# Decode attention with a K/V cache: TensorE's loop rotated by one PV, with a new order of loads at the start and of VectorE's work at the end

## Chip, cores, metric

One Trainium2 chip, one of its cores. The metric is the time of one execution on the device in microseconds (us), the median over several executions. The chip of the first comparison gave 660.2 us for the kernel before.

## The reference

A transformer block for one new token, batch 2: layer norm, attention with 32 heads of 128 over a cache of 8192 keys and values per head, a residual, then a gated feed-forward layer.

```
h  = x + attention(layernorm(x), k_cache, v_cache, wq, wo)    # caches: [2, 32, 8192, 128] bf16
h2 = h + ffn(layernorm(h), W_gate, W_up, W_down)              # 512 -> 1376 -> 512
```

The caches are 2 x 134 MB of the 281 MB that the kernel reads. Arithmetic is small: each byte of the cache is used once.

## The kernel before

The work is cut into 32 pairs (two heads of one batch entry each). For each pair one K load and one V load of 4 MB go into four slots of on-chip memory: K of even pairs in slot 0, V of even pairs in 1, K of odd pairs in 2, V of odd pairs in 3. The scores of a pair are computed by two engines. VectorE takes 96 of the 128 columns (one multiply `k_mult`, four halving adds `k_adds`, one reduce), TensorE the other 32 (`k_part`: transposes, which ScalarE evicts, then small matmuls). ScalarE makes the exponentials. `pv` multiplies them with V on TensorE and adds up two pairs in one PSUM bank; ScalarE evicts the bank, that is, copies the results out of PSUM (`sums`), `collect` picks the results out of it, and VectorE divides by the sum of the exponentials (`normalize`, `o_scale`) and spreads the result for the output projection (`o_spread`). TensorE, VectorE and ScalarE run 15 turns of a loop, each one even and one odd pair. The last two pairs (30 and 31) are a straight tail, followed by the feed-forward layer. SyncE issues the loads in program order, each when its slot is free.

TensorE's loop and tail, with cuts:

```python
with nc.Fori(0, NI, engines=OrderedEngineSet([nc.tensor.engine])):
    k_part(body, 0, (1, 2, 3, 4), ((k2p, 1),))
    collect(body, 6)
    pv(body, 0, ((JC, J, ((slot_sem[1], 16), (a2p, 5))), (0, JC, ((a2p, 7),))))
    k_part(body, 1, (8, 9, 10, 11), ((k2p, 2),))
    nc.tensor.wait_ge(l2p, 1)
    o_gather(body)
    nc.tensor.sem_inc(l2p, -1)
    pv(body, 1, ((JC, J, ((slot_sem[3], 16), (a2p, 12))), (0, JC, ((a2p, EV),))))
    z_sum(Ob)
    nc.tensor.sem_inc(slot_sem[1], -16)
    nc.tensor.sem_inc(slot_sem[3], -16)
    nc.tensor.sem_inc(k2p, -2)
    nc.tensor.sem_inc(a2p, -EV)
n_body = pe.count - body.base
pe.count = body.base + NI * n_body

tail = Tokens(0)
P0, P1 = NP - 2, NP - 1
collect(tail, 1)
t_ob_loop = (pe.sem, tail.at["ob"])
k_part(tail, P0, (2, 3, 4, 5), ((k2p, 1),))
nc.tensor.wait_ge(l2p, 1)
o_gather(tail)
nc.tensor.wait_ge(a2p, 7)
nc.tensor.wait_ge(sem_wo, 16)
for r in range(DR):
    i = nc.tensor.matmul(
        Op[1][32 * (r % 4):32 * (r % 4) + B, :], lhsT=O_all[:, r, :], rhs=X[:, r * D:(r + 1) * D],
        start=(r < 4), stop=(r >= DR - 4))
tail.mark("op", i)
nc.tensor.wait_ge(a2p, 9)
for c in range(DC):
    nc.tensor.matmul(
        Wp[:, c * B:(c + 1) * B], lhsT=os_sb[:].rearrange("p (n c) -> p c n", c=DC)[:, c, :], rhs=sel2[:],
        start=False, stop=False, skip_group_check=True)
k_part(tail, P1, (10, 11, 12, 13), ((k2p, 2),))
pv(tail, P0, ((JC, J, ((slot_sem[1], 16), (a2p, 6))), (0, JC, ((a2p, 8),))))
pv(tail, P1, ((V_LAST, J, ((sem_vl[0], 16), (a2p, 15))), (0, V_LAST, ((a2p, 15), (sem_vl[1], 16)))),
   lambda: tail.mark("z", z_sum(Sp[0])))
```

PV, and what VectorE does for the last two pairs (P0 = 30, P1 = 31):

```python
def pv(T, p, parts, between=None):
    s = (2 * p + 1) % 4
    v_t = tile(s)
    q = p % PG
    n = 0
    for j0, j1, waits in parts:
        if between and n:
            nc.tensor.wait_ge(*waits[0])
            between()
        for sem, val in waits:
            nc.tensor.wait_ge(sem, val)
        for j in range(j0, j1, VJ):
            c = 32 * (n % 4)
            i = nc.tensor.matmul(
                Op[0][c:c + 16, :], lhsT=e_t[q][:, j // VJ, :],
                rhs=v_t[:, j:j + VJ, :].rearrange("p j d -> p (j d)"),
                start=(q == 0 and n < 4), stop=(q == PG - 1 and n >= J // VJ - 4))
            if T is body and n == 0:
                T.mark(("fp", p), i)
            n += 1
    T.mark(("pv", p), i)
# ...
    if p >= P0:
        nc.vector.wait_ge(g2d, p - P0 + 1)
        nc.vector.wait_ge(slot_sem[s], 16)
        nc.vector.sem_inc(k2p, 1)
        dve.last()
        t_dm[p] = dve.run(k_mult(p))
        k_adds(p, dve.run, dve.last)
        if p == P0:
            dve.wait(tokp("pv", p - 2))
        t_s[p] = dve.run(k_reduce(p))
        if p == P0:
            dve.wait(t_ob_loop)
            normalize(Ob, dve.run, dve.last)
            o_spread(g - 1, dve, dve.run(o_scale()))
```

ScalarE's part for pair 30 and the loads of SyncE:

```python
    if p == P0:
        act.wait(tokp("pv", p - 1))
        sums()
        evacs()
        act.wait(tok("og", NI))
        to_pe(nc.scalar.activation(
            out=O_all[:].rearrange("p r b -> p b r"),
            in_=Op[1][:, 0:B * DR].rearrange("p (b r) -> p b r", r=DR), func=ACT.Copy))
        act.wait(t_s[p])
        exp_dve(p)
        act.wait(tok("op", NI))
        to_pe(nc.scalar.activation(out=os_sb[:], in_=Op[1][:], func=ACT.Copy))
    elif p == P1:
        evacs()
        act.wait(t_s[p])
        exp_dve(p)

    if p + 2 < NP:
        sp.wait((d2s, p + 1), tokp("kf", p))
        load(s, A_k_cache, p + 2)
    v_loads = [p] if p < NP - 5 else [NP - 5] if p == NP - 4 else [NP - 4, NP - 3] if p == NP - 3 else []
    for r in v_loads:
        sp.wait(tokp("pv", r))
        if r < NP - 3:
            load((2 * r + 1) % 4, A_v_cache, r + 2)
# ...
```

The softmax here doesn't subtract the row's maximum and nothing guards it: scores larger than these inputs give would overflow.

## Time and profile before

| | kernel before |
|---|---|
| time, median of 6 runs | 660.2 us (660.03 to 660.39) |
| bytes read | 281 MB |
| one turn of the loop | 38.86 us |
| DMA rate in the loop | 432 GB/s, share 1.00 |
| VectorE busy in a turn | 28.8 us |
| TensorE busy in a turn | 18.7 us |

The table of stretches of the kernel before gives, for a stretch of time, the busy time of each engine, the granted clock of TensorE as a share of full speed, the busy share of the 16 DMA engines and what they moved. The first line is the columns, then one turn, then 11 turns.

```profile
core 0: us, PE busy (x) PEld busy (x) DVE busy (x) ACT busy (x) POOL busy (x), PEclk, DMA share, GB/s
92.05:130.89 38.84, 18.74 (x174) 10.85 (x174) 28.78 (x15) 12.84 (x26) 4.53 (x7) 0.59 1.00 432
130.89:558.36 427.47, 207.78 (x1914) 120.59 (x1914) 316.65 (x165) 141.45 (x286) 49.88 (x77) 0.58 1.00 432
```

No compute engine is busy for more than three quarters of a turn, and DMA is never idle. The chain of waits in order of time (start, us, what) says the same: it is made of K loads, each followed only by the multiply that frees its slot.

```profile
286.46 6.57 DVE prod L540
...
293.10 32.09 DMA slot<-in_A_k_cache_dram
...
325.31 6.57 DVE prod L540
```

A load of 4 MB at this rate takes 9.72 us (38.86 / 4). The list of DMA issues of the same profile (size, then median us from issue to landing) shows that K loads land after 32.1 us, so more than three loads are under way at once (32.1 / 9.72 = 3.3):

```profile
slot<-in_A_k_cache_dram SPq DMA_DIRECT2D x32, 4096.0 KB, 32.1
slot<-in_A_v_cache_dram SPq DMA_DIRECT2D x31, 4096.0 KB, 30.3
```

From the timeline of the kernel before (start, us, engine, instruction, and in brackets how long the engine was idle before it and for whom):

```profile
612.68 6.56 DVE L540 TENSOR_TENSOR prod<-slot,q_c 128x12288 bf16<-128x12288 bf16 x1 [0.92 <-DVEq L603]
616.70 3.33 PE L405 MATMUL O<-slot,e 128*16 128x512 bf16 x32 [13.06 <-DMA slot<-in_A_v_cache_dram]
...
620.73 1.05 PE L417 MATMUL Ob<-sel,os_sb 128*128 128x4 f32 x8 [0.39 <-ACT os_sb L569]
...
626.92 0.16 DVE L503 TENSOR_REDUCE zr<-Ob 128x4 f32<-128x8 f32 x1
...
628.02 6.55 DVE L540 TENSOR_TENSOR prod<-slot,q_c 128x12288 bf16<-128x12288 bf16 x1
...
641.05 6.08 PE L405 MATMUL O<-slot,e 128*16 128x512 bf16 x56
...
641.37 0.95 DVE L554 TENSOR_REDUCE scores<-prod 128x96 f32<-128x768 bf16 x1
...
647.38 0.61 PE L405 MATMUL O<-slot,e 128*16 128x512 bf16 x8
...
648.69 1.05 PE L417 MATMUL Ob<-sel,os_sb 128*128 128x4 f32 x8 [0.70 <-ACT os_sb L569]
...
657.22 0.65 SPq L820 DMA_DIRECT2D out_dram<-kT  x1
```

TensorE stands idle for 13.06 us until V of pair 29 lands, then does that PV and the collect. VectorE meanwhile goes through pairs 30 and 31 without a pause: the collect is done at 621.8, but `normalize` comes only at 626.92, behind the reduce of pair 30, so nobody waits for it. PV of pair 30 and most of PV of 31 are one run of 56 matmuls.

### The profile page before, as it was taken

How to read it: one execution, taken by the hardware profiler on the slowest of the kernel's cores; microseconds unless marked ns; L12 is line 12 of the kernel's file. 1: busy time of each engine (PE TensorE's matmuls, PEld its weight loads, DVE VectorE, ACT ScalarE, POOL GpSimd, SP SyncE). 2: the span in 40 equal slices, each digit the busy share in tenths (PEclk: the TensorE clock that was granted, in tenths of full speed). 3: DMA queues.
4: the chain of work that ended last, by engine and by line, in shares of the span. 5: the costliest groups of instructions: out<-in, count | busy, mean ns of one | idle time of the engine just before them, and what ended most of it. 6: DMA issues, size and time to landing. Idle time of an engine off the chain costs nothing.

```text
span 659.2 us, 7582 instructions
## 1 busy us (share of the span) xinstructions
PE 324.3 (49%) x3073; PEld 188.6 (29%) x3073; DVE 469.2 (71%) x280; ACT 213.6 (32%) x431; POOL 73.5 (11%) x125
## 2 busy tenths in 40 slices
PE   2753454435455343655535364443556444354577
PEld 0331332213233121433313142221324222133344
DVE  1585576788767678776768877676886767787991
ACT  1622333143342223334223343422324332333250
POOL 3002002020200202020020201002020110202000
PEclk9856556565756657555665756756555765655656
DMA  8999999999999999999999999999999999999997
GB/s 366 444 437 431 420 445 416 443 428 431 438 422 441 422 439 433 428 435 424 441 422 439 433 428 433 426 441 422 439 434 426 435 424 441 424 437 433 428 417 295
DMA packets 10653, 281.17 MB, mean 427 GB/s; under 512 B 1202, under 2 KB 1300, under 8 KB 1812
## 3 DMA queue, kind: packets, MB, share of 16 engines
q1 hardware_dynamic: 10632, 281.06, 99.3%
q8 instruction: 5, 0.08, 0.1%
q14 instruction: 4, 0.03, 0.0%
q10 hardware_dynamic: 12, 0.00, 0.0%
HBM read 281.05 MB, written 0.00 MB: 426 GB/s over the span
## 4 chain that ended last, share of the span: by engine, by line
DMA 76%; DVE 19%; PE 4%; issue 1%; ACT 1%; SPq 0%; DVEq 0%
DMA slot<-in_A_k_cache_dram 76%; DVE prod L540 16%; DVE prod L549 2%; PE O L405 1%; PE O L463 1%; PE T L381 0%; ACT kT L566 0%; PE W L469 0%; DVE scores L554 0%; PE S L756 0%; PE O L756 0%; PE O L808 0%; PE Ob L417 0%; SPq L172 0%; PE S L364 0%
## 5 line engine op out<-in xcount | busy, mean ns | idle before, releaser
L540 DVE TENSOR_TENSOR prod<-slot,q_c 128x12288 bf16<-128x12288 bf16 x32 | 209.9, 6558 | 148.0 <-DMA slot<-in_A_k_cache_dram 141.3
L405 PE MATMUL O<-slot,e 128*16 128x512 bf16 x1024 | 119.3, 621 | 219.9 <-ACT e L495 146.2
L549 DVE TENSOR_TENSOR prod<-prod 128x6144 bf16<-128x6144 bf16 (+3 forms) x128 | 212.2, 1657 | 7.8
L566 ACT ACTIVATE kT<-T 128x1024 bf16<-128x1024 bf16 x128 | 126.1, 1022 | 144.6 <-PE T L381 141.9
L381 PE MATMUL T<-ident_f,slot 128*128 128x128 f32 x512 | 108.6, 365 | 29.1 <-DVEq L587 29.1
L405 PEld LDWEIGHTS O<-slot,e 128*16 128x16 bf16 x1024 | 26.4, 114 | 287.0 <-ACT e L495 172.9
L495 ACT ACTIVATE e<-scores 64x96 bf16<-64x96 f32 x64 | 19.5, 304 | 239.6 <-DVEq L601 238.9
L381 PEld LDWEIGHTS T<-ident_f,slot 128*128 128x128 f32 x512 | 79.0, 188 | 44.2 <-DVEq L587 43.3
L537 POOL COPY q_c<-q_all 128x136 bf16<-128x136 bf16 x32 | 57.2, 1788 | 195.5 <-DVEq L591 152.5
L364 PE MATMUL S<-q_c,kT 128*128 128x4 bf16 x1024 | 47.4, 168 | 40.8 <-ACT kT L566 40.0
L364 PEld LDWEIGHTS S<-q_c,kT 128*128 128x128 bf16 x1024 | 39.1, 104 | 67.9 <-ACT kT L566 66.8
L417 PE MATMUL Ob<-sel,os_sb 128*128 128x4 f32 x136 | 30.1, 345 | 24.2 <-ACT os_sb L569 24.2
L417 PEld LDWEIGHTS Ob<-sel,os_sb 128*128 128x128 f32 x136 | 28.6, 311 | 26.1 <-ACT os_sb L569 26.1
L520 POOL MEMSET O_l<- 128x40 bf16 (+1 forms) x13 | 1.8, 136 | 303.9 <-DVEq L598 303.9
L554 DVE TENSOR_REDUCE scores<-prod 128x96 f32<-128x768 bf16 x32 | 30.5, 953 | 2.8
L566 ACT ACT_TABLE_LOAD x15 | 19.2, 1283 | 0.3
L495 ACT ACTIVATE e<-S 64x32 bf16<-64x32 f32 x64 | 13.0, 202 | 15.1 <-PE S L364 14.7
L569 ACT ACTIVATE os_sb<-O 128x512 f32<-128x512 f32 x17 | 10.1, 597 | 12.8 <-PE O L405 12.4
L495 ACT ACTIVATION_READ_ACCUMULATOR e<-S 64x1 f32 x64 | 12.8, 201 | 0.7
L495 ACT ACTIVATION_READ_ACCUMULATOR e<-scores 64x1 f32 x64 | 11.8, 185 | 0.0
L426 PEld LDWEIGHTS Ob<-zs,ones_f 128*128 128x128 f32 x30 | 7.1, 296 | 12.5 <-issue 12.5
L525 POOL COPY rsel<-rows 128x30 bf16<-128x30 bf16 x28 | 5.9, 209 | 33.3 <-DVEq L598 32.5
(104 smaller groups left out, 90.6 us busy)
## 6 DMA issues: line engine op xcount, KB each, us to landing
slot<-in_A_k_cache_dram SPq DMA_DIRECT2D x32, 4096.0 KB, 32.1
slot<-in_A_v_cache_dram SPq DMA_DIRECT2D x31, 4096.0 KB, 30.3
slot<-in_A_wq_dram SPq DMA_DIRECT2D x1, 4096.0 KB, 12.2
X<-in_A_wo_dram SPq DMA_DIRECT2D x1, 3840.0 KB, 45.8
slot<-in_A_v_cache_dram SPq DMA_DIRECT2D x1, 3072.0 KB, 23.3
slot<-in_B_W_up_dram SPq DMA_DIRECT2D x1, 1376.0 KB, 23.2
slot<-in_B_W_gate_dram SPq DMA_DIRECT2D x1, 1376.0 KB, 26.2
slot<-in_A_v_cache_dram SPq DMA_DIRECT2D x1, 1024.0 KB, 25.4
```

Source lines behind the costliest of these rows:

```text
L364: i = nc.tensor.matmul(Sp[p % 2][:, 2 * jj:2 * jj + 4], lhsT=kv_[:, k, r, :], rhs=q_c[p % 2][:, 4 * r:4 * r + 4], start=(r == 0), stop=(r ...
L381: i = nc.tensor.transpose(Tp[g % 2][:, k * 128:(k + 1) * 128], k_t[:, j:j + 2, :].rearrange("p j d -> p (j d)").bitcast(F32), ident_f[:])
L405: i = nc.tensor.matmul(Op[0][c:c + 16, :], lhsT=e_t[q][:, j // VJ, :], rhs=v_t[:, j:j + VJ, :].rearrange("p j d -> p (j d)"), start=(q == ...
L417: i = nc.tensor.matmul(Ob[:, 0:4], lhsT=os_sb[:, jj * Dh:(jj + 1) * Dh], rhs=sel[:, 4 * jj:4 * jj + 4], start=(jj == 0), stop=(jj == VJ - 1))
L426: return nc.tensor.matmul(bank[:, ZC:ZC + 8], lhsT=ones_f[:], rhs=zs[:], start=True, stop=True)
L495: i = nc.scalar.activation(out=e_t[q][h, j0 // VJ:j1 // VJ, 8 * q:8 * q + 8].rearrange("p g (j a) -> p g j a", a=2)[:, :, :, a], in_=src(h ...
L537: nc.gpsimd.tensor_copy(out=q_c[p % 2][:], in_=q_all[:, p]).then_inc(g2d, 1)
L540: return nc.vector.tensor_tensor(out=prod[:, 0:JC, :], in0=tile((2 * p) % 4)[:, 0:JC, :], in1=q_c[p % 2][:, 8:QW].unsqueeze(1).broadcast_t ...
L549: run(nc.vector.tensor_tensor(out=prod[:, 0:JC, 0:w], in0=prod[:, 0:JC, 0:w], in1=prod[:, 0:JC, w:2 * w], op=ALU.add))
L554: return nc.vector.tensor_reduce(out=scores[p % PG][:, 0:JC], in_=prod[:, 0:JC, 0:8], axis=AX.X, op=ALU.add)
L566: to_pe(nc.scalar.activation(out=kT[gg % 2][:], in_=Tp[gg % 2][:].bitcast(BF16), func=ACT.Copy))
L569: to_pe(nc.scalar.activation(out=os_sb[:], in_=Op[0][:], func=ACT.Copy))
```

## The change

The intent: TensorE should not hold up K of the next even pair by PV of the odd pair. So the loop begins with the sum and K of the even pair, and only then does PV of the odd pair of the turn before, its eviction and the collect. In the first turn that PV works on zeros (e is zero, slot 3 still holds wq, the sums are set to 1), so the result is not used. The slot of odd V is freed later, and the second V load is issued only in the first turn; wo is issued ahead of it. In the tail K of pair 30 also comes ahead of PV of 29, and VectorE does `normalize` and the spread behind its first add of pair 30, so that TensorE gets the spread early. Core of the diff, with cuts:

```diff
@@ -203,7 +203,11 @@
                     pool.run(nc.gpsimd.affine_select(
                         out=mask[:], in_=mask[:], pattern=[[2 * sgn, DR // 2], [-DR * sgn, NM]],
                         compare_op=ALU.is_ge, fill=0.0, base=base, channel_multiplier=sgn))
-                t_const = pool.run(nc.gpsimd.memset(zs[:], 0.0))
+                pool.run(nc.gpsimd.memset(zs[:], 0.0))
+                pool.last()
+                for a in range(2):
+                    t_const = pool.run(nc.gpsimd.memset(zs[64 * a:64 * a + 64, a:4:2, :], 1.0))
+                    pool.last()
                 dve.wait(t_id)
                 t_ident = dve.run(nc.vector.tensor_copy(out=ident[:], in_=ident_f[:]))
                 for bank in Op:
@@ -297,8 +301,6 @@
                     out=rows[:, 0:128 - 4 * DR], in0=rows[:, 0:128 - 4 * DR], in1=ident[:, 4 * DR:], op=ALU.max))
                 dve.last()
                 t_sel = dve.run(nc.vector.tensor_copy(out=rows[:, DR:], in_=rows[:, 0:DR]))
-                sp.wait(t_q)
-                load(3, A_v_cache, 1)
                 nc.sync.dma_start(
                     X[:], A_wo[0:128 * DR].rearrange("(p r) n -> p (r n)", r=DR)).then_inc(sem_wo, 16)
 
@@ -337,6 +339,7 @@
                 nc.tensor.matmul(Ob[:, 0:ZC + 8], lhsT=onesn[:], rhs=ident[:, 0:ZC + 8], start=True, stop=True)
 
                 EV = 13
+                nc.tensor.sem_inc(slot_sem[3], 16)
 
                 class Tokens:
 
... (pv and collect take the argument `done`, for whom they count)
@@ -434,15 +443,17 @@
                     T.mark("og", i)
 
                 with nc.Fori(0, NI, engines=OrderedEngineSet([nc.tensor.engine])):
-                    k_part(body, 0, (1, 2, 3, 4), ((k2p, 1),))
-                    collect(body, 6)
-                    pv(body, 0, ((JC, J, ((slot_sem[1], 16), (a2p, 5))), (0, JC, ((a2p, 7),))))
-                    k_part(body, 1, (8, 9, 10, 11), ((k2p, 2),))
+                    nc.tensor.wait_ge(a2p, 1)
+                    z_sum(Ob)
+                    k_part(body, 0, (2, 3, 4, 5), ((k2p, 1),))
+                    pv(body, 1, ((JC, J, ((slot_sem[3], 16),)), (0, JC, ())), done=p2a)
+                    collect(body, 7, ("pv", 1))
+                    pv(body, 0, ((JC, J, ((slot_sem[1], 16), (a2p, 6))), (0, JC, ((a2p, 8),))))
+                    k_part(body, 1, (9, 10, 11, 12), ((k2p, 2),))
                     nc.tensor.wait_ge(l2p, 1)
                     o_gather(body)
+                    nc.tensor.wait_ge(a2p, EV)
                     nc.tensor.sem_inc(l2p, -1)
-                    pv(body, 1, ((JC, J, ((slot_sem[3], 16), (a2p, 12))), (0, JC, ((a2p, EV),))))
-                    z_sum(Ob)
                     nc.tensor.sem_inc(slot_sem[1], -16)
                     nc.tensor.sem_inc(slot_sem[3], -16)
                     nc.tensor.sem_inc(k2p, -2)
@@ -452,12 +463,15 @@
 
                 tail = Tokens(0)
                 P0, P1 = NP - 2, NP - 1
-                collect(tail, 1)
+                nc.tensor.wait_ge(a2p, 1)
+                z_sum(Ob)
+                k_part(tail, P0, (2, 3, 4, 5), ((k2p, 1),))
+                pv(tail, P0 - 1, ((JC, J, ((slot_sem[3], 16),)), (0, JC, ())))
+                collect(tail, 7)
                 t_ob_loop = (pe.sem, tail.at["ob"])
-                k_part(tail, P0, (2, 3, 4, 5), ((k2p, 1),))
                 nc.tensor.wait_ge(l2p, 1)
                 o_gather(tail)
-                nc.tensor.wait_ge(a2p, 7)
+                nc.tensor.wait_ge(a2p, 8)
                 nc.tensor.wait_ge(sem_wo, 16)
                 for r in range(DR):
                     i = nc.tensor.matmul(
@@ -469,9 +483,9 @@
                     nc.tensor.matmul(
                         Wp[:, c * B:(c + 1) * B], lhsT=os_sb[:].rearrange("p (n c) -> p c n", c=DC)[:, c, :], rhs=sel2[:],
                         start=False, stop=False, skip_group_check=True)
-                k_part(tail, P1, (10, 11, 12, 13), ((k2p, 2),))
-                pv(tail, P0, ((JC, J, ((slot_sem[1], 16), (a2p, 6))), (0, JC, ((a2p, 8),))))
-                pv(tail, P1, ((V_LAST, J, ((sem_vl[0], 16), (a2p, 15))), (0, V_LAST, ((a2p, 15), (sem_vl[1], 16)))),
+                k_part(tail, P1, (11, 12, 13, 14), ((k2p, 2),))
+                pv(tail, P0, ((JC, J, ((slot_sem[1], 16), (a2p, 10))), (0, JC, ())))
+                pv(tail, P1, ((V_LAST, J, ((sem_vl[0], 16), (a2p, 16))), (0, V_LAST, ((a2p, 16), (sem_vl[1], 16)))),
                    lambda: tail.mark("z", z_sum(Sp[0])))
 
                 def tok(key, g):
... (tokens renumbered; k_adds split into single adds)
@@ -614,6 +631,8 @@
                         nc.scalar.wait_ge(p2a, n_a)
                         exp_pe(q)
                         if q == 0:
+                            n_a += 1
+                            nc.scalar.wait_ge(p2a, n_a)
                             sums()
                         nc.scalar.wait_ge(d2a, q + 1)
                         exp_dve(q)
@@ -635,14 +654,14 @@
                         nc.vector.sem_inc(k2p, 1)
                         dve.last()
                         t_dm[p] = dve.run(k_mult(p))
-                        k_adds(p, dve.run, dve.last)
-                        if p == P0:
-                            dve.wait(tokp("pv", p - 2))
-                        t_s[p] = dve.run(k_reduce(p))
+                        dve.last()
+                        k_add(Dh // 2, dve.run)
                         if p == P0:
                             dve.wait(t_ob_loop)
                             normalize(Ob, dve.run, dve.last)
                             o_spread(g - 1, dve, dve.run(o_scale()))
+                        k_adds(p, dve.run, dve.last, Dh // 2)
+                        t_s[p] = dve.run(k_reduce(p))
 
                     if p < P1:
                         if p % 2 == 0:
@@ -664,22 +683,25 @@
                         exp_pe(p)
 
                     if p == P0:
+                        evacs()
                         act.wait(tokp("pv", p - 1))
                         sums()
-                        evacs()
                         act.wait(tok("og", NI))
                         to_pe(nc.scalar.activation(
                             out=O_all[:].rearrange("p r b -> p b r"),
                             in_=Op[1][:, 0:B * DR].rearrange("p (b r) -> p b r", r=DR), func=ACT.Copy))
+                        act.wait(tok("op", NI))
+                        to_pe(nc.scalar.activation(out=os_sb[:], in_=Op[1][:], func=ACT.Copy))
                         act.wait(t_s[p])
                         exp_dve(p)
-                        act.wait(tok("op", NI))
-                        to_pe(nc.scalar.activation(out=os_sb[:], in_=Op[1][:], func=ACT.Copy))
                     elif p == P1:
                         evacs()
                         act.wait(t_s[p])
                         exp_dve(p)
 
+                    if p == 0:
+                        sp.wait(tok(("pv", 1), 0))
+                        load(3, A_v_cache, 1)
                     if p + 2 < NP:
                         sp.wait((d2s, p + 1), tokp("kf", p))
                         load(s, A_k_cache, p + 2)
```

More of the change, by code (lines that the diff above doesn't have):

```diff
@@ L390, in k_part, with pv @@
                     score(NG - 1)
-                def pv(T, p, parts, between=None):
+                def pv(T, p, parts, between=None, done=None):
                     s = (2 * p + 1) % 4
@@ L407, in pv, with collect @@
                                 rhs=v_t[:, j:j + VJ, :].rearrange("p j d -> p (j d)"),
-                                start=(q == 0 and n < 4), stop=(q == PG - 1 and n >= J // VJ - 4))
-                            if T is body and n == 0:
+                                start=(q == 0 and n < 4), stop=(q == PG - 1 and n >= J // VJ - 4),
+                                skip_group_check=True)
+                            if T is body and n == q == 0:
                                 T.mark(("fp", p), i)
                             n += 1
-                    T.mark(("pv", p), i)
-                def collect(T, a):
+                    if done:
+                        i.then_inc(done, 1)
+                    else:
+                        T.mark(("pv", p), i)
+                def collect(T, a, done=None):
                     nc.tensor.wait_ge(a2p, a)
@@ L419, in collect @@
                             rhs=sel[:, 4 * jj:4 * jj + 4], start=(jj == 0), stop=(jj == VJ - 1))
+                        if done and jj == 0:
+                            T.mark(done, i)
                     if T is body:
@@ L483, in tokp @@
                 def tokp(kind, p, *g):
-                    return tok(kind if kind == "og" else (kind, p) + g, p // 2)
+                    return tok(kind if kind == "og" else (kind, p) + g, (p + (kind == "pv")) // 2)
                 def to_pe(inst):
@@ L542, in k_mult, with k_add, k_adds @@
                         in1=q_c[p % 2][:, 8:QW].unsqueeze(1).broadcast_to([128, JC, Dh]), op=ALU.mult)
-                def k_adds(p, run, last):
-                    w = Dh
+                def k_add(w, run):
+                    run(nc.vector.tensor_tensor(
+                        out=prod[:, 0:JC, 0:w], in0=prod[:, 0:JC, 0:w], in1=prod[:, 0:JC, w:2 * w], op=ALU.add))
+                def k_adds(p, run, last, w=Dh):
                     while w > 8:
@@ L548, in k_adds @@
                         last()
-                        run(nc.vector.tensor_tensor(
-                            out=prod[:, 0:JC, 0:w], in0=prod[:, 0:JC, 0:w], in1=prod[:, 0:JC, w:2 * w], op=ALU.add))
+                        k_add(w, run)
                     last()
@@ L605, in program @@
                 act.wait(t_const)
+                nc.scalar.sem_inc(a2p, 1)
                 with nc.Fori(0, NI, engines=OrderedEngineSet([nc.scalar.engine])):
@@ L713, in program @@
                 sums()
-                collect(tail, 16)
+                collect(tail, 17)
                 dve.wait(tok("ob", NI))
```

## The prediction

> **What bounds the kernel now.** The DMA queue. The table of stretches shows the 16 DMA engines busy for a share of 1.00 at 432 GB/s from 92.05 to 626.40 us. The timeline shows one turn of the loop (two K and two V loads, 16.78 MB) every 38.86 us: 16.78 MB / 38.86 us = 432 GB/s, one 4 MB load per 9.72 us. [...] The chain of waits is 76% K loads. Compute has room: in a turn DVE is busy 28.8 us, PE 18.7, ACT 12.8. The queue is deep: a K load lands 32.1 us and a V load 30.3 us after its issue (DMA issues), so about 3.2 loads are under way.
>
> **What the change does.** It moves no byte away (281 MB). It adds one dummy PV of 32 matmuls in the first turn (about 3.5 us of PE, idle anyway) and two small memsets. In the loop PE no longer has to do the odd pair's PV before the next K: but in the trace that PV ends at 304.45, before K lands at 305.8, so the wait removed was not on the chain.
>
> What it costs: the odd V's buffer comes free later. Measured from the even K's landing: K part 6.2 us, PV 3.5, eviction 0.6, then the load is issued: about +10.5 us, where it was issued 1.3 us before. SP issues in order, so the next K goes out at 10.9 instead of 6.7. At 10.5 the next K still has 8.9 us to transfer (it lands at 19.4), so the queue is shallower but not dry, and landings stay 9.72 us apart. DVE's normalize needs the collect (estimate: done at 12.5) after its adds (13.4): no stall. The loop stays at 38.86 us.
>
> Start: wo goes ahead of the second V, which is issued at about 38 us instead of 16.7. By then 21 MB are queued, enough until about 53 us. The same bytes, no gap.
>
> Tail: K of pair 30 now comes before PV of 29 (13.1 us of PE waiting for V become useful), but DVE, after its first add of pair 30 (about 622.6), waits for PV 29 (ends about 622.5), the eviction (0.6) and the collect (1.1): it stalls about 2 us in the middle of its work. The multiply of pair 31 moves from 628.0 to about 630, its reduce's end from 642.3 to about 644.4, exp to 645.2, and the last PV (24 matmuls, sum, 8 matmuls) from 648.0 to about 649.1. DMA ends at about 655 as before, in time. After the last PV everything is a serial chain of 11 us.
>
> **Prediction.** 660.2 + 1.1 = 661.3 us, 8 in 10 between 659.7 and 663.3. Faster by over 2%: 0.01; within 2%: 0.96; slower: 0.03. Below 659 it cannot fall unless DMA speeds up.
>
> **What would show it.** Loop: 38.86 us per turn, DMA share 1.00 at 432 GB/s; V's time from issue to landing falls to about 25 us in the median (18 to 19 for odd pairs), K's to about 30; PV matmuls 1056 instead of 1024; waits of the queue's issuer for PV rise. Tail: a DVE stall of 1.5 to 3 us before normalize near 623; the last PV ends near 649. Start: landings unchanged from the third K on.
>
> **What would make it wrong.** The queue runs dry in each turn because PE, eviction and collect are slower than read, or because DMA loses rate when only one load waits behind the running one: each us lost per turn costs 15 us (+2.3%). Or the tail's stall hides because PE, not DVE, sets the last PV: then 660.

660.2 us, the measured time, plus 1.1 us for the last PV (648.0 to about 649.1), gives 661.3 us. The floor of 659 us is the author's estimate and was not shown; the lowest time in any run here is 660.03 us.

## The result, and the profile after

| | runs | median | lowest to highest |
|---|---|---|---|
| kernel before | 6 | 660.17 us | 660.03 to 660.39 |
| changed kernel | 6 | 662.11 us | 660.31 to 663.06 |

The ratio is 1.0024, with a 95% interval of 1.0008 to 1.0041. Ratios here are the mean time of one kernel's runs over that of the other's of the same rounds, so not quite the ratio of the medians quoted. The change is within 2%, and it is slower. The spread is new: 0.4 us became 2.8 us.

The loop of the changed kernel, in the table of stretches (columns as before) from K to K:

```profile
92.27:131.13 38.86, 20.14 (x174) 12.53 (x174) 28.79 (x15) 12.98 (x26) 4.54 (x7) 0.50 1.00 432
131.13:558.57 427.44, 204.71 (x1914) 124.47 (x1914) 316.69 (x165) 141.90 (x286) 49.90 (x77) 0.57 1.00 432
```

The turns are as long as before to a hundredth of a microsecond. The timeline of one turn shows the rotation at work:

```profile
306.04 1.97 PE L384 MATMUL T<-ident_f,slot 128*128 128x128 f32 x8 [3.46 <-DVEq L603]
...
312.17 3.59 PE L408 MATMUL O<-slot,e 128*16 128x512 bf16 x32
...
317.07 0.33 SPq L172 DMA_DIRECT2D slot<-in_A_v_cache_dram  x1
317.45 0.43 SPq L172 DMA_DIRECT2D slot<-in_A_k_cache_dram  x1
```

The odd V's load goes out at 317.07, which is 11.0 us after K's multiply began at 306.07; before, one went out at 304.57, 1.3 us ahead of it. The next K goes out behind it, at 317.45; before, at 312.54. The two DMA issues of these lines land after 18.0 and 27.4 us, those of the even V and the odd K after 29.6 and 32.1 us. The list of DMA issues of the whole kernel gives the mixture:

```profile
slot<-in_A_k_cache_dram SPq DMA_DIRECT2D x32, 4096.0 KB, 30.0
slot<-in_A_v_cache_dram SPq DMA_DIRECT2D x31, 4096.0 KB, 29.6
```

And the tail of the changed kernel, to be read against the one above:

```profile
612.87 6.56 DVE L554 TENSOR_TENSOR prod<-slot,q_c 128x12288 bf16<-128x12288 bf16 x1 [0.92 <-DVEq L619]
...
619.40 3.59 PE L408 MATMUL O<-slot,e 128*16 128x512 bf16 x32
...
623.70 1.87 PE L424 MATMUL Ob<-sel,os_sb 128*128 128x4 f32 x8 [0.70 <-ACT os_sb L585]
...
625.60 0.17 DVE L517 TENSOR_REDUCE zr<-Ob 128x4 f32<-128x8 f32 x1 [2.78 <-PE Ob L424]
...
631.07 6.56 DVE L554 TENSOR_TENSOR prod<-slot,q_c 128x12288 bf16<-128x12288 bf16 x1
...
644.43 0.95 DVE L570 TENSOR_REDUCE scores<-prod 128x96 f32<-128x768 bf16 x1
...
646.32 2.74 PE L408 MATMUL O<-slot,e 128*16 128x512 bf16 x24 [3.40 <-ACT e L509]
...
649.39 0.61 PE L408 MATMUL O<-slot,e 128*16 128x512 bf16 x8
```

VectorE, which had never waited here, waits 2.78 us for the collect between two adds of pair 30. Its multiply of pair 31 starts at 631.07 instead of 628.02 and its last reduce at 644.43 instead of 641.37. TensorE in turn waits 3.40 us for the last exponentials, and the last PV ends at 650.00 (649.39 + 0.61) instead of 647.99: 2.0 us, which is the whole difference of the two spans (661.2 against 659.2). About 1 us of VectorE's 3 is hidden, because before PV of pair 31 had to queue behind that of pair 30.

The first collect, the same eight instructions, lasts 1.05 us before and 1.87 us after. The granted clock goes with it. Before:

```profile
615.00:618.00 3.00, 1.30 (x16) 0.47 (x20) 3.00 (x1) 0.00 (x0) 0.00 (x0) 0.50 0.93 396
618.00:621.00 3.00, 2.61 (x29) 1.10 (x21) 2.96 (x2) 0.60 (x1) 0.00 (x0) 0.73 1.04 448
621.00:624.00 3.00, 2.32 (x26) 2.09 (x26) 2.96 (x2) 1.68 (x2) 0.00 (x0) 0.84 0.91 393
```

After:

```profile
615.00:618.00 3.00, 2.74 (x27) 2.07 (x26) 3.00 (x1) 2.39 (x3) 0.00 (x0) 0.50 0.97 410
618.00:621.00 3.00, 2.23 (x32) 1.08 (x36) 2.96 (x2) 1.83 (x5) 0.00 (x0) 0.50 1.06 459
621.00:624.00 3.00, 2.30 (x22) 0.74 (x14) 1.82 (x1) 0.60 (x1) 0.00 (x0) 0.50 0.91 393
624.00:627.00 3.00, 1.71 (x12) 1.62 (x11) 1.21 (x9) 0.00 (x0) 0.00 (x0) 0.50 1.07 459
```

The third number from the right is the clock. Before, the collect (620.73 to 621.78) lay in the stretches at 0.73 and 0.84, after (623.70 to 625.57) in two at 0.50. That gave the theory to test.

In the traces of these two executions the clock is either 0.50 or 1.00, and each of the 35 stays recorded between two changes lasts a whole multiple of 3.41 us (3.41 to 71.7 us before, 3.41 to 112.6 us after). What raises or lowers it the two traces do not show. Before, it goes up at 619.63, down at 623.04, up at 646.94 and down at 650.35; in the changed kernel it goes down at 604.83, up at 642.37 and down at 645.78. Where this grid of 3.41 us lies differs from execution to execution: the two times at which the clock goes up, 619.63 and 642.37, are 6.66 steps apart. A value such as 0.84 is the mean of a stretch with a change in it: the first collect ran wholly at full clock (1.00) before and wholly at half clock (0.50) after.

### The profile page after: what moved, and what is told of

It is laid out like the page before. It is cut to its first block, busy times and chain, and to the rows that moved or that the text cites. A ratio compares the mean times of both kernels' runs of the same rounds, so it can differ in the third digit from the quotient of the medians.

```text
span 661.2 us, 7624 instructions
## 1 busy us (share of the span) xinstructions
PE 327.5 (50%) x3107; PEld 197.3 (30%) x3107; DVE 469.4 (71%) x280; ACT 214.2 (32%) x431; POOL 73.1 (11%) x127
## 4 chain that ended last, share of the span: by engine, by line
DMA 76%; DVE 19%; PE 3%; ACT 1%; issue 1%; SPq 0%; DVEq 0%; ACTq 0%
DMA slot<-in_A_k_cache_dram 76%; DVE prod L554 16%; DVE prod L559 3%; PE O L408 1%; PE Ob L424 0%; DVE scores L570 0%; PE T L384 0%; ACT kT L582 0%; PE S L778 0%; PE O L778 0%; PE O L830 0%; ACT e L509 0%; ACT os_sb L585 0%; PE S L367 0%; SPq L172 0%
## 5 line engine op out<-in xcount | busy, mean ns | idle before, releaser
L384 PE MATMUL T<-ident_f,slot 128*128 128x128 f32 x512 | 119.6, 394 | 66.2 <-DVEq L603 66.2
L408 PE MATMUL O<-slot,e 128*16 128x512 bf16 x1056 | 116.9, 607 | 54.7 <-ACT e L509 54.7
L384 PEld LDWEIGHTS T<-ident_f,slot 128*128 128x128 f32 x512 | 87.5, 204 | 81.2 <-DVEq L603 80.4
L435 PE MATMUL Ob<-zs,ones_f 128*128 128x8 f32 x32 | 9.5, 370 | 143.1 <-ACT e L509 143.1
L408 PEld LDWEIGHTS O<-slot,e 128*16 128x16 bf16 x1056 | 29.8, 118 | 113.1 <-ACT e L509 62.1
L367 PEld LDWEIGHTS S<-q_c,kT 128*128 128x128 bf16 x1024 | 40.5, 105 | 64.9 <-ACT kT L582 63.5
L424 PEld LDWEIGHTS Ob<-sel,os_sb 128*128 128x128 f32 x136 | 23.8, 263 | 26.5 <-ACT os_sb L585 26.5
L424 PE MATMUL Ob<-sel,os_sb 128*128 128x4 f32 x136 | 25.2, 309 | 11.9 <-ACT os_sb L585 11.9
## 6 DMA issues: line engine op xcount, KB each, us to landing
slot<-in_A_v_cache_dram SPq DMA_DIRECT2D x31, 4096.0 KB, 29.6
```

The lines of the kernel that those rows point to most:

```text
L367: i = nc.tensor.matmul(Sp[p % 2][:, 2 * jj:2 * jj + 4], lhsT=kv_[:, k, r, :], rhs=q_c[p % 2][:, 4 * r:4 * r + 4], start=(r == 0), stop=(r ...
L384: i = nc.tensor.transpose(Tp[g % 2][:, k * 128:(k + 1) * 128], k_t[:, j:j + 2, :].rearrange("p j d -> p (j d)").bitcast(F32), ident_f[:])
L408: i = nc.tensor.matmul(Op[0][c:c + 16, :], lhsT=e_t[q][:, j // VJ, :], rhs=v_t[:, j:j + VJ, :].rearrange("p j d -> p (j d)"), start=(q == ...
L424: i = nc.tensor.matmul(Ob[:, 0:4], lhsT=os_sb[:, jj * Dh:(jj + 1) * Dh], rhs=sel[:, 4 * jj:4 * jj + 4], start=(jj == 0), stop=(jj == VJ - 1))
L435: return nc.tensor.matmul(bank[:, ZC:ZC + 8], lhsT=ones_f[:], rhs=zs[:], start=True, stop=True)
```

## The experiments

The theory, T: the loop and the start cost nothing; the tail lost its slack. VectorE now waits in mid-work for a chain on TensorE (K of 30, PV of 29, eviction, collect), and how long that chain takes depends on which of its two values the clock has then (the collect alone: 1.05 us at 1.00, 1.87 us at 0.50). The rival, R: the time, or the spread, comes from the loop or the start, where the loads are issued later. All runs below gave the reference's result. The kernel before ran beside them on the same chip: 660.57 us for the first four experiments (660.26 to 660.87), 660.40 for the second four (660.08 to 660.74).

### The changed kernel again

> The changed kernel unaltered, for its spread and a second trace. Theory T (the tail's stall depends on the phase of TensorE's clock: K of pair 30, PV of 29 and the collect run at half or at full clock from run to run): times in two clumps again, about 660.3 and 662 to 663, median 661 to 662.5; in a trace of a 663 run DVE waits about 2.8 us before normalize near 623 and the collect's 8 matmuls take 1.87 us; in a trace of a 660.3 run the collect takes about 1.05 us and the wait is under 1 us. Rival R (the spread comes from the DMA in the loop): a slow trace then has turns longer than 38.86 us and the K of pair 29 lands later than 597.5.

No edit. Measured: 663.44 us (661.63 to 664.25, 6 runs), ratio 1.0042 (1.0030 to 1.0054). In the trace, an execution of 662.96 us, the turns are unchanged and R's slow loads are not there. But the expectation for a run near 663 was wrong in its detail: the first collect was quick (1.06 us) and VectorE waited 1.97 us. The rest was lost at another place:

```profile
645.41 2.74 PE L408 MATMUL O<-slot,e 128*16 128x512 bf16 x24 [3.55 <-ACT e L509]
648.08 0.60 PE L435 MATMUL S<-zs,ones_f 128*128 128x8 f32 x2
648.60 1.03 PE L408 MATMUL O<-slot,e 128*16 128x512 bf16 x8
...
650.34 1.87 PE L424 MATMUL Ob<-sel,os_sb 128*128 128x4 f32 x8 [0.70 <-ACT os_sb L585]
```

The last eight matmuls of PV take 1.03 us instead of 0.61 and the last collect 1.87 us instead of 1.05. So a second part was added to T: VectorE's delay leaves TensorE idle for about 3.5 us ahead of the last PV, and the last chain then may run at half clock too, as it did here (0.50 in every stretch from 639 to 654). Before, the clock went up at 646.94, within the run of 56 matmuls (641.05 to 647.13), and both were quick. That the pause decides it is a guess: in the first trace of the changed kernel TensorE paused for 3.40 us there, and both were quick too (0.61 and 1.05 us).

### Normalize behind the reduce again

> Undo only the place of normalize and spread in the tail: they come again after the reduce of pair 30, so the adds no longer wait for the collect. T: no DVE stall, the reduce of pair 31 ends near 642.5, time 660.0 to 660.6 in every run (spread under 0.5 us), 1.5 us below the changed kernel's median. Rival R (the time is lost in the loop or at the start): 661.5 to 662.5 stays.

```diff
                         k_add(Dh // 2, dve.run)
+                        k_adds(p, dve.run, dve.last, Dh // 2)
+                        if p == P0:
+                            dve.wait(tokp("pv", p - 2))
+                        t_s[p] = dve.run(k_reduce(p))
                         if p == P0:
                             dve.wait(t_ob_loop)
                             normalize(Ob, dve.run, dve.last)
                             o_spread(g - 1, dve, dve.run(o_scale()))
-                        k_adds(p, dve.run, dve.last, Dh // 2)
-                        t_s[p] = dve.run(k_reduce(p))
```

The wait for PV of pair 28 had to come back with it: in the changed kernel the wait for the collect covers it, and without either the race check finds the reduce writing scores that the exponentials may still read. Measured: 660.23 us (660.07 to 660.47), ratio to the kernel before 0.9996 (0.9983 to 1.0009). The rotated loop, the new start and the new order of TensorE's tail are all still in it. The trace shows that the collect was slow here too, and that it cost nothing:

```profile
623.56 1.87 PE L424 MATMUL Ob<-sel,os_sb 128*128 128x4 f32 x8 [0.70 <-ACT os_sb L585]
...
626.09 0.95 DVE L570 TENSOR_REDUCE scores<-prod 128x96 f32<-128x768 bf16 x1
...
626.96 0.16 DVE L517 TENSOR_REDUCE zr<-Ob 128x4 f32<-128x8 f32 x1
```

It ends at 625.43, before VectorE asks for it at 626.96. R is refuted: with the loop and the start as changed, moving normalize alone takes the loss away.

### Normalize between the last add and the reduce

> Normalize and spread between the last add and the reduce of pair 30. T: the collect is done (625.6 at half clock) before the adds are (626.1), so no stall, and the gather starts 1 us earlier than with normalize after the reduce: 659.5 to 660.3, small spread; the end is then close to the DMA's end (about 656) plus 3.5 us. R: 661.5 to 662.5.

```diff
                         k_add(Dh // 2, dve.run)
+                        k_adds(p, dve.run, dve.last, Dh // 2)
                         if p == P0:
                             dve.wait(t_ob_loop)
                             normalize(Ob, dve.run, dve.last)
                             o_spread(g - 1, dve, dve.run(o_scale()))
-                        k_adds(p, dve.run, dve.last, Dh // 2)
                         t_s[p] = dve.run(k_reduce(p))
```

Measured: 660.29 us (660.15 to 660.48), ratio 0.9997 (0.9984 to 1.0010). No stall, as expected, but the further gain hoped for did not come. The trace suggests why: now TensorE waits for loads.

```profile
646.29 0.61 PE L408 MATMUL O<-slot,e 128*16 128x512 bf16 x8 [0.79 <-DMA slot<-in_A_v_cache_dram]
...
652.83 1.71 PE L778 MATMUL O<-d_b,slot 128*128 128x2 bf16 x44 [0.58 <-DMA slot<-in_B_W_gate_dram]
```

The last part of V and then W_gate come off the queue, which is full to the end (DMA share 0.96 to 1.04 in each stretch of 3 us from 642 to 654). So with the compute chain this short, the end of the DMA is probably the limit (no run tests it), and no version here is faster than the kernel before by more than the noise.

### The clock raised by dummy work

> The changed kernel plus 24 dummy matmuls (128x512) on TensorE's idle 603 to 612 us ahead of the tail's sum, result not used. T: the clock is granted in full when the tail begins, K of pair 30 ends near 618 and the collect near 621.5 (1.05 us for its 8 matmuls), before DVE's first add is done at 622.7: no stall, 660.0 to 660.8 in every run. If the clock is not what matters (R, or the stall is set by waits only): 661.5 to 663 as the changed kernel.

```diff
+                nc.tensor.wait_ge(sem_wo, 16)
+                for r in range(24):
+                    nc.tensor.matmul(Tp[0][:], lhsT=ident[:], rhs=X[:, r * D:(r + 1) * D], start=True, stop=True)
                 nc.tensor.wait_ge(a2p, 1)
                 z_sum(Ob)
```

Everything of the change is in, VectorE's early wait too. Measured: 660.37 us (660.29 to 661.43), ratio 1.0005 (0.9992 to 1.0017). The profiled execution (660.29 us), stretches and timeline:

```profile
612.00:615.00 3.00, 1.93 (x16) 1.20 (x15) 2.08 (x2) 1.90 (x6) 0.00 (x0) 1.00 1.09 470
615.00:618.00 3.00, 2.17 (x40) 1.61 (x40) 3.00 (x1) 2.72 (x3) 0.00 (x0) 1.00 0.93 396
618.00:621.00 3.00, 2.30 (x42) 1.09 (x38) 2.97 (x2) 1.41 (x5) 0.00 (x0) 1.00 1.05 451
```

```profile
618.09 1.90 PE L408 MATMUL O<-slot,e 128*16 128x512 bf16 x32
...
620.69 1.05 PE L424 MATMUL Ob<-sel,os_sb 128*128 128x4 f32 x8 [0.70 <-ACT os_sb L588]
...
622.82 0.16 DVE L520 TENSOR_REDUCE zr<-Ob 128x4 f32<-128x8 f32 x1
```

The dummy matmuls begin near 605: TensorE is busy for 1.23 us of the stretch of 3 us from 603 and for all of the next two. The clock is 0.50 in the stretch from 606 and 0.92 in that from 609, so it is up from about 609.5. PV of 29 takes 1.90 us instead of 3.59, the collect is done at 621.74, and VectorE does not wait. More work on TensorE made the kernel 3 us faster (660.37 against 663.44 us on the same chip). Two of the five runs took 661.22 and 661.43, which the expectation excluded; they were not profiled. The last chain of the tail is still behind a TensorE pause in this kernel (3.26 us in the trace, up to the landing of a V load), so the clock there is a likely cause, but that is not shown.

### Control: dummy work too little or too early

> Control of the run with 24 dummy matmuls: only 6 of them, done near 606, some 6 us before the tail begins. If it is the clock at the tail's start that the 24 changed, these 6 change nothing: the clock is at 0.5 again by 612, DVE waits 2 to 2.8 us, 661.5 to 664 as the changed kernel. If any dummy work (or the order of instructions it brings) does it: 660.0 to 660.8.

The same edit with `range(6)`. Measured: 663.72 us (663.07 to 663.89), ratio 1.0049 (1.0036 to 1.0062). The dummy matmuls end at 608.3 (the expectation said near 606), the clock is at 0.50 in every stretch of 3 us from 603 to 627, and both places are slow: VectorE waits 2.78 us, the last eight matmuls of PV take 1.03 us and the last collect 1.87 us. So it is the clock at the start of the tail and not the added instructions that the 24 matmuls changed. This execution also shows the full price of the change: output issued at 660.53 against 657.22 before, 3.3 us.

### TensorE's tail in the old order

> The rotated loop kept, but in the tail PV of 29, its eviction and the collect come ahead of K of pair 30 again, as in the kernel before; normalize stays between the adds. T: the collect is done near 621.8, before DVE's first add of pair 30 (622.7): no stall, 660.0 to 660.8, spread under 0.6 us. Rival R (the rotation of the loop itself or the start costs the time): 661.5 to 664.

```diff
                 z_sum(Ob)
-                k_part(tail, P0, (2, 3, 4, 5), ((k2p, 1),))
                 pv(tail, P0 - 1, ((JC, J, ((slot_sem[3], 16),)), (0, JC, ())))
-                collect(tail, 7)
+                collect(tail, 2)
                 t_ob_loop = (pe.sem, tail.at["ob"])
+                k_part(tail, P0, (3, 4, 5, 6), ((k2p, 1),))
... (ScalarE: sums ahead of evacs again)
```

Measured: 660.35 us (660.28 to 660.71), ratio 1.0001 (0.9988 to 1.0014). With PV of 29 and the collect ahead of K of 30, the collect is done at 622.19 and VectorE's early normalize at 622.70 no longer waits. So the loss needs both halves of the new tail: K ahead of PV on TensorE, and the early wait on VectorE. Either alone is free.

### The order of loads at the start

> Undo only the order of loads at the start: wo is issued right behind the second V instead of ahead of it. All theories but one: the queue holds 17 MB until about 44 us and the second V is issued at 38, so no gap; K of pair 3 lands near 92.3 and the time is that of the changed kernel, 661.5 to 664. If the start's order costs anything: a gap in DMA share before 60 us or another landing of K of pair 3, by as much as the time changes.

```diff
-                nc.sync.dma_start(
-                    X[:], A_wo[0:128 * DR].rearrange("(p r) n -> p (r n)", r=DR)).then_inc(sem_wo, 16)
...
                         load(3, A_v_cache, 1)
+                        nc.sync.dma_start(
+                            X[:], A_wo[0:128 * DR].rearrange("(p r) n -> p (r n)", r=DR)).then_inc(sem_wo, 16)
```

Measured: 662.96 us (660.38 to 663.77, 6 runs), ratio 1.0036 (1.0021 to 1.0050): the changed kernel's time and spread. K of pair 3 ends its wait at 92.0 us in the chain (50.84 + 41.19), as before. Undoing the start's order changes nothing that shows above the spread.

### The odd V issued later still

> The odd V's load is issued only behind PV of the even pair (about 18.9 us after the even K landed, instead of 10.5). Claim to test: in the changed kernel the queue is shallower but still has room of 8.9 us, so the loop costs nothing. If so, this kernel eats it: at 19.4 the running load ends, [...]so each turn grows from 38.86 to about 40.2 to 40.8 us and 13 or 14 turns add 18 to 27 us: 678 to 690. If the queue's depth has nothing to do with it: 661.5 to 664.

```diff
-                    collect(body, 7, ("pv", 1))
+                    collect(body, 7)
                     pv(body, 0, ((JC, J, ((slot_sem[1], 16), (a2p, 6))), (0, JC, ((a2p, 8),))))
+                    body.at[("pv", 1)] = body.at[("pv", 0)]
```

Measured: 689.37 us (688.88 to 689.60, 4 runs), ratio 1.044 (1.0425 to 1.0455). A turn takes 40.8 us. The chain of waits of this kernel has K loads that begin at 425.75 and, four turns later, at 588.96. In the loop DMA falls to a share of 0.97:

```profile
92.27:597.43 505.16, 220.10 (x2140) 134.03 (x2140) 359.56 (x186) 159.48 (x324) 57.91 (x85) 0.59 0.97 411
```

The hole is visible in the stretches around one late issue (at 336.90 us):

```profile
336.00:337.00 1.00, 0.86 (x9) 0.00 (x0) 0.00 (x0) 0.00 (x0) 0.00 (x0) 0.50 0.01 0
337.00:338.00 1.00, 0.54 (x3) 0.54 (x4) 0.50 (x1) 0.00 (x0) 0.00 (x0) 0.50 0.71 197
```

That load lands after 12.3 us, where the transfer alone takes 9.72: the rest, about 2.6 us by this estimate, is no longer hidden behind another load. So the claim holds: what protects the loop of the changed kernel is the load still running when the next is issued. The rotation used up 12 us of this depth for nothing; 8 us more and it would have cost 4%.

### Three more looks at the changed kernel

> Looks at the changed kernel, to catch an execution near 660.4 in a trace. T: if the profiled run is under 661, its clock was granted in full for part of 612 to 625 us, its collect's 8 matmuls take about 1.05 us, and the end of the wait of DVE before normalize is near 623, not 625.6; if it is over 662.5, the clock was at 0.5 there, or in the last PV and collect near 645 to 652.

> A second look at the changed kernel, expected as in after_look1: under 661 only with the clock granted in full in part of 612 to 625 us and DVE's wait ending near 623; over 662.5 with the clock at 0.5 there or near 645 to 652.

> A third look at the changed kernel, expected as in after_look1: under 661 only with the clock granted in full in part of 612 to 625 us and DVE's wait ending near 623; over 662.5 with the clock at 0.5 there or near 645 to 652.

Measured: 663.20, 663.89 and 662.86 us (single runs, state unknown); 660.63 for the kernel before. None was an execution under 661, so the first half of the expectation stays untested. The second half held: in all three the last eight matmuls of PV took 1.03 us and the last collect 1.87 us, and in the second the first collect was slow as well.

The clock's grid sorts the first collect. Take the seven traces of the table below without the kernel before, and the two with normalize moved: all nine have K of 30 ahead of PV of 29, and none has the 24 dummy matmuls. In five of them the clock goes up between 622.74 and 623.35, ahead of the collect, and the collect takes 1.05 or 1.06 us. In the other four it is at 0.50 in every stretch of 3 us from 612 to 627, and the collect takes 1.87 us. The run with the later V, whose first collect lies 26 us later, agrees: the clock goes up at about 648.85 (0.86 in the stretch from 648 to 651), and the collect at 649.68 takes 1.07 us in the chain.

The profiled executions of the changed kernel, of the run with the old order of loads and of the control together, all in us:

| profiled execution | time | VectorE's wait before normalize | first collect | last 8 matmuls of PV | last collect |
|---|---|---|---|---|---|
| kernel before | 660.49 | none | 1.05 | 0.61 | 1.05 |
| changed | 662.40 | 2.78 | 1.87 | 0.61 | 1.05 |
| changed, wo behind V | 662.83 | 1.97 | 1.05 | 1.03 | 1.87 |
| changed, third look | 662.86 | 1.94 | 1.05 | 1.03 | 1.87 |
| changed, again | 662.96 | 1.97 | 1.06 | 1.03 | 1.87 |
| changed, first look | 663.20 | 1.97 | 1.05 | 1.03 | 1.87 |
| control with 6 matmuls | 663.65 | 2.78 | 1.87 | 1.03 | 1.87 |
| changed, second look | 663.89 | 2.79 | 1.87 | 1.03 | 1.87 |

One slow collect gives 662.4 to 663.2, two give 663.7 to 663.9. Open: an execution of the changed kernel near 660.4 (2 of 15 in all) was not caught in a trace, so that both places are quick in it is inferred from the run with 24 dummy matmuls. Quick collects alone would not be enough: as an estimate, 662.96 less 0.42 and 0.82 us is about 661.7, near the runs at 661.63 and 661.82. For 660.4 VectorE's wait has to go as well. None of these executions was traced.

## Why the prediction was right

The time (662.1 us) lies in the range (659.7 to 663.3), and the sign was right. That the time lies in the range was partly luck: the same kernel, in the six runs of a later round, had a median of 663.44 us, just outside. The mechanism does not hang on that. Point by point:

- **"The loop stays at 38.86 us."** Right: 38.86 us, DMA at 432 GB/s. The odd V lands 18.0 us after its issue ("18 to 19") and K's median is 30.0 us ("about 30"). V's median is 29.6 and not "about 25": the loads are half at 18.0 and half at 29.6, and a median of two groups is no mean. PV matmuls are 1056, as predicted. The late-V run shows that the reason given (depth of the queue) is the right one.
- **"Start: ... no gap."** Right; the run with the other order changes nothing.
- **"DVE ... stalls about 2 us in the middle of its work."** The mechanism is right and shown by undoing either half of it. Its size was 1.94 to 2.79 us.
- **"the eviction (0.6) and the collect (1.1)"** is the term that was mis-sized. 1.1 us was read from the kernel before, where the collect ran at full clock (1.00). In the profiled execution of the changed kernel it took 1.87 us at 0.50. PV of 29 was taken to end at 622.5 and ended at 623.0. So the last PV ended at 650.0 and not 649.1, and 660.2 + 1.1 became 660.2 + 2.0.
- **"After the last PV everything is a serial chain of 11 us."** Right in the profiled execution (650.0 to 661.2), but in the other four traces of the changed kernel its collect is 0.8 us longer. The prediction said nothing of a spread. That TensorE would pause ahead of the last PV (3.40 and 3.55 us in two traces), and that the clock there can be 0.50 or 1.00, was not considered.

The change's intent failed earlier: the wait that the rotation removes was not on the chain. Before, PV of the odd pair ended at 304.52 (301.79 + 2.73), 1.4 us before K's multiply began at 305.89.

## What to carry to other kernels

Where DMA is busy all the time, as here (share 1.00 at 432 GB/s), a new order of the compute has next to nothing to win and its slack to lose (the orders tried here came to 0.9996 to 1.044 of the time before): reckon first what the bytes cost, and treat the rest as slack to be kept. An engine that is asked to wait in the middle of its own work needs a producer that is surely done by then, so place the wait by the producer's slow case; on TensorE that is here the duration at half clock (1.87 us for the collect), and a duration read where the clock was up (1.05 us) is the fast case. A new spread among runs is itself a finding: here it was the first sign that the end had come to depend on where the clock's changes fall.

## What the traces leave open

- What raises the clock. In the changed kernel TensorE was busy for 2.15, 2.74, 2.23 and 2.30 of each 3 us from 612 to 624, and by the trace even for the whole 3.41 us from 632.13 to 635.54, about half of it small fp32 matmuls and half transposes; the clock stayed at 0.50 until 642.37. With the 24 bf16 matmuls back to back it was up from about 609.5, with 6 it was at 0.50 from 603 to 627. Whether the density of the work or the kind of instruction makes the difference, no run here separates.
- The quick end of the spread. The changed kernel, whose chain of waits has no slack, took 660.3 to 664.3 us, the kernel before, where the chain has slack, 660.0 to 660.9; no execution of the changed kernel near 660.4 was traced.
- SyncE's last load (96 KB) took 2.39 us to issue before, 4.55 in the changed kernel and 7.03 with the 24 matmuls, and each ended between 630.6 and 630.9 us, however early it began (628.22, 626.26, 623.84); most other issues take 0.3 to 0.5 us. Why it waits until then was not tested.
